# Two kinds of attention layer, interleaved: layer A's weights loaded whole, used in place, and packed into strips on the chip

## The chip, the core and the metric

The program runs on one core of one Trainium2 chip. The core has TensorE (PE, with its weight loads shown as PEld), VectorE (DVE), ScalarE (ACT), GpSimd (POOL) and SyncE (SP); each engine works through its own list of instructions in order. SP, ACT and POOL can issue transfers (DMA). The metric is the device time of one execution in microseconds (us). The time given is the median of three runs; the profile is that of one further execution, with its own time.

## The reference

The input `x` has 2048 rows of 576. Four residual layers follow each other, A, B, A, B, each on a layernorm of `x`; both A layers have the same weights, and both B layers too.

```python
# A: 32 heads of 18, each row attends to itself and 7 earlier rows, 2 apart
qkv = x @ wqkv                                   # 576 x 1728
idx = pos[:, None] - (arange(8) * 2)[None, :]    # masked where < 0
logits = einsum('bhsd,bhswd->bhsw', q, k[idx]) * 18 ** -0.5
o = einsum('bhsw,bhswd->bhsd', softmax(logits), v[idx])
out = o @ wo                                     # 576 x 576

# B: 32 heads of 128, segments of 32 rows, one after the other
mem = mem0                                       # 8 x 576
for s in range(64):
    h = concatenate([mem, xs])                   # 40 rows
    q, k, v = h @ Wq, h @ Wk, h @ Wv             # each 576 x 32 x 128
    p = softmax(mask(q @ k.T * 128 ** -0.5))     # memory sees all, rows are causal
    o = (p @ v) @ Wo                             # 32 x 128 x 576
    mem = o[:8]                                  # the next segment needs it
    outs.append(o[8:])

x = x + A(layernorm(x)); x = x + B(layernorm(x))
x = x + A(layernorm(x)); x = x + B(layernorm(x))
```

B is a recurrence: a segment's memory rows are the output of the one before.

## The kernel before

**Tiling.** The data stand transposed: features on the partitions (576 = 4 x 128 + 64, so five chunks), rows on the free axis. A works in tiles of 64 rows (`T`), B in segments of 32. Layers 1 (A) and 3 (A) and the two B layers run interleaved: step `t` of B computes segment `t` of the first B layer (lane 0) and segment `t - 5` of the second (lane 1) in the same matmuls, for 69 steps. Before a step, `trace` calls `a_tile` for the A tiles that have come due: first tile 0 alone, then tiles 1 and 2 as a pair (the "twin"), then tile 3, and from then on a tile of layer 1 with a tile of layer 3.

**Weights.** Wq, Wk and Wv of B stay in SBUF (`Wb`): 4 chunks of 128 features in a large tile each, the remaining 64 features of Wq and Wk in `wqk_r` (Wq on partitions 0 to 63, Wk on 64 to 127), those of Wv in `wv_r`. B's output weights stay in `wo`. A's weights have no tile of their own. They are used as ten strips, `[P, 5 * 256]` each: 0 to 5 are the columns of q, k and v, 6 the last 64 columns of each of the three, 7 to 9 the output projection. As long as B's output weights have not been loaded, `wo` holds the first copy of the strips ("kept", at `i * 1280`). `wload` gives a tile its strip: the first time by a gather from `A_wqkv` or `A_wo` (`L516` on SP for the four chunks, `L517` on ACT for the remainder), the second time from `wo` where it is a strip of q, k, v; later in one of two `ring` buffers, up to the third time by a gather again, which is then written to DRAM as one piece (`strips[i]`, L529), and from then on by one transfer from there (L521).

**The start.** `setup` makes the identity and the masks on POOL and the zeros on DVE. `prologue` then lists B's weight loads, all on POOL: `wqk_r` twice, the halves of Wq and Wk, those of Wv, `wv_r` twice, and `wo` in four pieces of 8 heads. The pieces of `wo` wait until what is kept there has been used. Each tile of A goes through `a_input` (load of 64 rows of x to the one buffer `x0` on SP, L660; transpose on PE, L665), `layernorm` (sums by a matmul with ones, L476; statistics on DVE; logarithm and exponential on ACT, L489 and L490), 14 blocks of projection (five matmuls each, L580), `a_attend` (products of q and k, sums over a head's 18 features by matmul, L697; softmax; spread of the weights by matmul, L722; products with v and sums), and `a_out` (L766), which adds to x, stores it, and leaves the second layernorm's result for B in `xnb`. The memory rows `mem0` are loaded to the same `x0` on SP (L448), and transposed (L452).

**A step of B.** `load_x` copies a segment to `hT`. `qk` computes q and k for the heads of a group `QG` (6, 6, 4, 6, 6, 4 heads): per head and matrix four matmuls of 128 features (L930), and one for the remaining 64. For groups in `HM` these last ones are a separate operation, in which q's and k's matmuls each use one half of the rows of the array (L949); in the other groups they are full-height matmuls (L938), in which the half that is not wanted meets zeros in `hT`. `HM` lists all six groups. `vpass` computes V (L993), `scores` the scores of 16 heads (L1034, L1038, L1044) and the softmax (`nmx`, exponential, `sum`, then a transpose to `pt`, L884), `pv` p times V (L1085), `oproj` the output (L1109), `mem_out` puts the memory rows into the next step's `hT`, and `x_out` adds to x.

**Who decides the order.** None of this is issued as it is called. `_Plan.op` records each operation with the engines that may do it, an assumed duration, a priority, what it waits for, and the buffers it takes. `_Plan.run` then plays through time with these durations, and each time an engine is free it takes the ready operation with the lowest priority number; the order so found is the order in each engine's list. On the chip an engine waits for what its next instruction needs, whatever else is ready. The priorities are numbers of `PR`; `at(t)` picks variants with `_e` or `_l` for the first 12 and last 8 steps where `PR` has them (it has none). The plan also charges 0.097 us for a change of the array's tile shape (`SWITCH`), and assumes when the weights land:

```python
return pl.op("POOL", 0.8, ..., prio, lat=max(3.0, 6.5 + mbs[0] / 0.36 - begin))
```

Of the kernel before, what the change touches and what calls it, by code (L numbers as in the profile page):

```python
# [16 lines left out]
P = 128  # L17
# [19 lines left out]
HM = ((0, 1, 2, 3, 4, 5), (0, 1, 2, 3, 4, 5))  # L37
# [11 lines left out]
class _Op:  # L49
    __slots__ = ("eng", "us", "lat", "fn", "prio", "seq", "acq", "uses", "wait", "next", "mode", "tmin", "done", "lk", "mm")  # L50


class _Plan:
# [10 lines left out]
    START = {"POOL": 8.4, "DVE": 2.5, "ACT": 2.2, "SP": 0.8}  # L64
# [190 lines left out]
class _K:  # L255
# [17 lines left out]
    def at(self, t):  # L273
        x = "_e" if t < EARLY else "_l" if t >= self.nsteps - LATE else ""
        return {k: PR.get(k + x, v) for k, v in PR.items() if k[-2:] not in ("_e", "_l")}

# [20 lines left out]
    def setup(self):  # L297
# [13 lines left out]
        self.sel(ident[:], [[-1, P]], 1, 0, ALU.is_equal, 0.0)  # L311
        self.ones = ones = cp.tile([P, P], BF16, name="ones")
# [25 lines left out]
        self.Wb = []  # L338

        qkr = cp.tile([P, NH * P], BF16, name="wqk_r")  # L340
        for nm in ("wq", "wk", "wv"):
            self.Wb.append((cp.tile([P, 4, NH * P], BF16, name=nm), cp.tile([P, (NH // 2) * P], BF16, name="wv_r") if nm == "wv" else qkr))
        self.wo = wo = cp.tile([P, NH * D + 64], BF16, name="wo")
# [52 lines left out]
        nc.vector.memset(wo[64:128, 0:9 * 1280].rearrange("p (a b) -> p a b", b=1280)[:, :, 1024:1280], 0.0)  # L396
        nc.vector.memset(wo[:, 6 * 1280:7 * 1280].rearrange("p (k n) -> p k n", n=256)[:, :, 192:256], 0.0)
        nc.vector.memset(wo[:, 9 * 1280:9 * 1280 + 640], 0.0)
# [13 lines left out]

    def prologue(self):
# [8 lines left out]
        mbs = [2.65]  # L422

        def load(out, in_, mb, begin, prio=-50.0):
            mbs[0] += mb
            return pl.op("POOL", 0.8, lambda e: nc.gpsimd.dma_start(out=out, in_=in_), prio, lat=max(3.0, 6.5 + mbs[0] / 0.36 - begin))
        src = (self.B_Wq, self.B_Wk, self.B_Wv)
        self.w_in = [[None] * 2 for _ in range(3)]
        n = 0
        for i in range(2):  # L430
            load(self.Wb[i][1][i * 64:(i + 1) * 64, :], src[i][512:576].rearrange("p h e -> p (h e)"), 0.52, 9.2 + 0.8 * n)
            n += 1
        for ws in ((0, 1), (2,)):
            for hf in range(2):
                for i in ws:
                    self.w_in[i][hf] = load(self.Wb[i][0][:, :, hf * 2048:(hf + 1) * 2048], src[i][0:512, hf * 16:(hf + 1) * 16].rearrange(
                        "(k p) h e -> p k (h e)", k=4), 2.1, 9.2 + 0.8 * n)
                    n += 1
        for hf in range(2):
            o = load(self.Wb[2][1][hf * 64:(hf + 1) * 64, :], src[2][512:576, hf * 16:(hf + 1) * 16].rearrange("p h e -> p (h e)"),  # L440
                     0.26, 9.2 + 0.8 * n)
            n += 1
        self.vr_in = o
        self.wo_in = [load(self.wo[:, n * 8 * D:(n + 1) * 8 * D].rearrange("p (h d) -> p h d", h=8),
                           self.B_Wo[n * 8:(n + 1) * 8].rearrange("h e d -> e h d"), 1.18, 36.0, -8.0) for n in range(4)]
# [49 lines left out]
    def wload(self, i, prio, dep):  # L495
# [3 lines left out]
        self.strip_n[i] = k = self.strip_n.get(i, -1) + 1  # L499
        kept = k == 0 or k == 1 and i < 7  # L500
        w = None if kept else pl.buf("ring")
        src = self.A_wqkv if i < 7 else self.A_wo
        if i < 6:
            cols = ((i // 2 * D + i % 2 * 256, 256),)
        elif i == 6:
# [19 lines left out]
        if kept:  # L525
            return view, (), self.firsts[i]
# [756 lines left out]
```

## Time and profile before

| | us |
|---|---|
| median of the runs (2100.57 to 2102.97) | 2101.82 |
| the profiled execution | 2115.16 |
| its span, first to last instruction | 2113.4 |
| PE busy in the span | 1994.7 |
| DVE busy | 1588.8 |
| ACT busy | 1094.1 |
| POOL busy | 761.8 |

Busy times are those of the profiled execution. Matmuls are pipelined, so that PE counts as busy from the first to the last of a run of them; 59,850 matmuls make its 1994.7 us. The page of the profile cuts the span in 40 equal slices and gives a digit for each, the tenths that an engine was busy. A line of the timeline has the start, the duration, the engine and source line, what is written from what, and in brackets how long the engine had been idle and what ended that. Of a transfer, the queue shows when it was issued; it lands later.

### The profile page before, as it was taken

The numbers are of one execution on the slowest core, as the hardware profiler recorded it, in microseconds if no ns is written. First come the engines' busy times: TensorE is split into PE (matmuls) and PEld (weight loads), VectorE is DVE, ScalarE is ACT, GpSimd is POOL, SyncE is SP. The second block draws the span as 40 slices with busy tenths as digits, with TensorE's granted clock in tenths as the row PEclk, the third lists the DMA queues.
The fourth block names the chain that finished last, engine by engine and source line by source line (L and its number), as shares of the span: only waits on it lengthen the run. The fifth ranks groups of instructions, "written<-read, shape, count | busy, mean of one in ns | idle before, by whom it ended". The sixth has DMA issues, their size and how long they took to land.

```text
span 2113.4 us, 130329 instructions
## 1 busy us (share of the span) xinstructions
PE 1994.7 (94%) x59850; PEld 1662.0 (79%) x59850; DVE 1588.8 (75%) x4055; ACT 1094.1 (52%) x2847; POOL 761.8 (36%) x1089
## 2 busy tenths in 40 slices
PE   0689999999999999999999999999999999999987
PEld 0567788888888888888888888887878888888776
DVE  2677778778877787778777777878777877776574
ACT  0444555555555555555555555555555555555443
POOL 2333434343343344343343433443434433322320
PEclk9889999999999999999999999999999999999998
DMA  9432222222212222222222222222222222222120
GB/s 317 140 105 58 76 78 77 72 63 70 68 55 69 78 78 76 59 76 61 56 66 78 78 77 67 68 71 59 62 70 79 77 72 62 70 68 68 58 68 10
DMA packets 92631, 161.65 MB, mean 76 GB/s; under 512 B 14632, under 2 KB 49712, under 8 KB 91952
## 3 DMA queue, kind: packets, MB, share of 16 engines
q1 hardware_dynamic: 86544, 134.14, 21.7%
q0 software_dynamic: 4576, 18.88, 2.7%
q8 instruction: 467, 7.65, 1.5%
q14 instruction: 84, 0.69, 0.1%
q10 hardware_dynamic: 960, 0.30, 0.1%
HBM read 137.32 MB, written 15.96 MB: 73 GB/s over the span
## 4 chain that ended last, share of the span: by engine, by line
PE 79%; DVE 13%; DMA 3%; issue 3%; ACT 1%; SPq 0%; DVEq 0%; POOL 0%; ACTq 0%
PE r L930 21%; PE r L1109 18%; PE r L993 17%; PE r L580 6%; DVE xn L294 4%; PE r L949 4%; PE r L1085 3%; DVE big L294 3%; PE r L766 2%; PE r L476 2%; PE r L1044 1%; DMA x<-in_B_mem_dram 1%; DVE qk L289 1%; PE r L1038 1%; PE r L697 1%
## 5 line engine op out<-in xcount | busy, mean ns | idle before, releaser
L930 PE MATMUL r<-hT,wq 128*128 128x80 bf16 (+1 forms) x8832 | 616.9, 199 | 3.4 <-issue 1.6
L930 PE MATMUL r<-hT,wk 128*128 128x80 bf16 (+1 forms) x8832 | 615.2, 199 | 0.8 <-issue 0.4
L287 ACT ACTIVATE qk<-r 128x480 bf16<-128x480 f32 (+3 forms) x610 | 267.3, 496 | 460.7 <-PE r L949 453.7
L930 PEld LDWEIGHTS <-wq 128*128 128x128 bf16 x8832 | 446.5, 100 | 28.3 <-issue 19.7
L930 PEld LDWEIGHTS <-wk 128*128 128x128 bf16 x8832 | 448.0, 100 | 1.1 <-issue 1.0
L1109 PE MATMUL r<-OT,wo 128*128 128x80 bf16 (+1 forms) x11040 | 407.8, 200 | 9.7 <-ACT OT L287 5.5
L1109 PEld LDWEIGHTS <-wo 128*128 128x128 bf16 x11040 | 394.2, 100 | 28.0 <-issue 26.0
L993 PE MATMUL r<-wv,hT 128*32 128x512 bf16 x5376 | 356.3, 383 | 3.0 <-ACT hT L287 2.3
L294 POOL TENSOR_TENSOR ex<-ex,sum 128x320 bf16<-128x320 bf16 x138 | 109.3, 792 | 593.2 <-DVE sum L874 571.6
L993 PEld LDWEIGHTS <-hT 128*32 128x32 bf16 x6720 | 164.2, 96 | 140.0 <-issue 5.2
L294 POOL TENSOR_TENSOR big<-qT,kT 128x1024 bf16<-128x1024 bf16 (+1 forms) x154 | 254.9, 1670 | 21.9 <-DVE kT L289 13.6
L294 POOL TENSOR_TENSOR big<-big 128x640 bf16<-128x640 bf16 (+1 forms) x68 | 101.6, 1494 | 358.7 <-DVE big L294 256.8
L287 ACT ACTIVATE V<-r 128x512 bf16<-128x512 f32 x275 | 164.6, 599 | 121.3 <-PE r L993 115.6
L287 ACT ACTIVATE big<-r 128x384 bf16<-128x384 f32 (+1 forms) x318 | 121.6, 437 | 136.6 <-PE r L722 135.4
L287 ACT ACTIVATE OT<-r 128x320 bf16<-128x320 f32 (+1 forms) x380 | 138.5, 422 | 88.1 <-PE r L1085 87.8
L289 DVE CAST qk<-r 128x480 bf16<-128x480 f32 (+2 forms) x218 | 122.2, 575 | 65.2 <-PE r L949 63.1
L580 PE MATMUL r<-xn,ring 128*128 128x128 bf16 (+1 forms) x2310 | 159.6, 216 | 3.2 <-issue 2.9
L863 DVE TENSOR_REDUCE nmx<-r 128x8 f32<-128x320 f32 x276 | 133.4, 483 | 32.9 <-PE r L1038 31.1
L864 DVE TENSOR_TENSOR r<-r,nmx 128x320 f32<-128x320 f32 x276 | 137.9, 500 | 9.5
L580 PEld LDWEIGHTS <-ring 128*128 128x128 bf16 x2310 | 124.7, 98 | 25.5 <-issue 15.4
L993 PE MATMUL r<-wv_r,hT 128*32 128x512 bf16 x1344 | 133.3, 380 | 0.0
L289 DVE CAST OT<-r 128x320 bf16<-128x320 f32 (+1 forms) x172 | 75.6, 461 | 71.3 <-PE r L1085 71.2
(150 smaller groups left out, 3050.3 us busy)
## 6 DMA issues: line engine op xcount, KB each, us to landing
ring<-strip SPq DMA_DIRECT2D x288, 320.0 KB, 3.2
x1T<-x SPq DMA_DIRECT2D x32, 160.0 KB, 4.3
x<-x1T SPq DMA_DIRECT2D x32, 160.0 KB, 3.0
ring<-strip SPq DMA_DIRECT2D x32, 160.0 KB, 2.3
x3T<-x SPq DMA_DIRECT2D x32, 160.0 KB, 3.3
x<-x3T SPq DMA_DIRECT2D x32, 160.0 KB, 3.9
wo<-in_B_Wo_dram POOLq DMA_DIRECT2D x4, 1152.0 KB, 8.5
wq<-in_B_Wq_dram POOLq DMA_DIRECT2D x2, 2048.0 KB, 20.7
```

Source lines behind the costliest of these rows:

```text
L287: nc.scalar.activation(out=out, in_=in_, func=ACT.Copy, scale=1.0 if scale is None else scale)
L289: (nc.vector if e == "DVE" else nc.gpsimd).tensor_copy(out=out, in_=in_)
L294: (self.nc.vector if e == "DVE" else self.nc.gpsimd).tensor_tensor(out=out, in0=in0, in1=in1, op=op)
L476: nc.tensor.matmul(psf, lhsT=(self.ones if c < 4 else self.ones_h)[:, :], rhs=xs.t[:, c].rearrange("p a t -> p (a t)"), start=(c == 0), st ...
L580: nc.tensor.matmul(ps.t[:, c * n:(c + 1) * n], lhsT=view()[:, kc, w0:w0 + P], rhs=xn.t[:, kc, 0:n], start=(kc == 0), stop=(kc == 4))
L863: nc.vector.tensor_reduce(out=m, in_=v, axis=AX.X, op=ALU.max, negate=True)
L864: nc.vector.tensor_tensor(out=v, in0=v, in1=m.unsqueeze(len(shp) - 1).to_broadcast(shp), op=ALU.add)
L930: nc.tensor.matmul(view(ps[wi])[:, hh], lhsT=self.Wb[wi][0][:, kc, h * P:(h + 1) * P], rhs=hT.t[:, kc, a:b], start=(hh == 0 and kc == 0), ...
L949: nc.tensor.matmul(view(ps[wi])[:, hh], lhsT=self.Wb[0][1][q2, h * P:(h + 1) * P], rhs=hT.t[q2, 4 + wi, a:b], start=False, stop=(hh == n - ...
L993: nc.tensor.matmul(ps.t[c * 32:(c + 1) * 32, :], lhsT=l, rhs=w, start=(kc == 0), stop=(kc == 4))
L1085: nc.tensor.matmul(ps[c].t[:, i * n + a - c0:i * n + z - c0], lhsT=V[b].t[q4, r, i, :], rhs=pt.t[q4, i, b, a:z], start=(i == 0 and b == bl ...
L1109: nc.tensor.matmul(psY.t[:, mb * W80 + c0:mb * W80 + c1], lhsT=self.wo[:, w0:w0 + P], rhs=self.OT[:, h % 16 // 4 * 8 + h // 16 * 4 + h % 4 ...
```

## The change

- `setup` makes the weight tiles before the masks, and `head` issues B's first four loads (both of `wqk_r`, the first halves of Wq and Wk) right after the identity, ahead of the masks on POOL.
- `whole` loads A's two weight matrices by four transfers on SP into `wo`, in rows of all columns, at 0 and from `WO0`. `slab` gives a tile its weights from there for the first and second use of each strip. The last 64 columns of q and k are copied side by side to `WR0` by DVE.
- `pack` copies each strip from there into a ring buffer, on POOL or DVE, and writes it to `strips[i]`. From the third use on, a strip comes from DRAM by one transfer; the gathers are gone.
- `load` lists the remaining weight loads, each in the plan only after the one eight places before has landed. The first two and the last pieces of `wo` wait for the strips packed out of them.
- `HM` has the groups 0, 1, 3 and 4, so that the groups 2 and 5 run their last 64 features at full height.
- `PR` has new numbers, and variants for tiles before the steps (`_i`), the first 5 steps (`_s`), the first 12 (`_e`) and the last 8 (`_l`). Copies of halos, some sums and products may take another engine in the first five tiles (`early`).

```diff
-HM = ((0, 1, 2, 3, 4, 5), (0, 1, 2, 3, 4, 5))
+HM = [[0, 1, 3, 4], [0, 1, 3, 4]]
...
-        x = "_e" if t < EARLY else "_l" if t >= self.nsteps - LATE else ""
-        return {k: PR.get(k + x, v) for k, v in PR.items() if k[-2:] not in ("_e", "_l")}
+        x = "_i" if t < 0 else "_s" if t < FIRST else "_e" if t < EARLY else "_l" if t >= self.nsteps - LATE else ""
+        return {k: PR.get(k + x, v) for k, v in PR.items() if k[-2:-1] != "_"}
...
         self.sel(ident[:], [[-1, P]], 1, 0, ALU.is_equal, 0.0)
...
+        self.loads = []
+        self.head()
...
+    def head(self):
+        self.mbs = 2.65
+        for i, w in ((0, self.B_Wq), (1, self.B_Wk)):
+            self.nc.gpsimd.dma_start(out=self.Wb[i][1][i * 64:(i + 1) * 64, :], in_=w[512:576].rearrange("p h e -> p (h e)"))
+            self.loads.append(0.52)
+        for i in range(2):
+            out, in_ = self.w_src(i, 0)
+            self.nc.gpsimd.dma_start(out=out, in_=in_)
+            self.loads.append(2.1)
...
+    def load(self, out, in_, mb, prio=-50.0):
+        pl, n = self.pl, len(self.loads)
+        end = self.landing(mb)
+        before = self.loads[n - 8] if n >= 8 else None
+        gate = pl.op("NONE", 0.0, None, prio, [before])
+        o = pl.op("POOL", 0.8, lambda e: self.nc.gpsimd.dma_start(out=out, in_=in_), prio, [gate], lat=3.0)
...
+        for i in range(10):
+            o = self.pack(i)
+            for n in ((0, 1) if i < 7 else (3,)):
+                pl.after(self.wo_in[n].issue, o)
...
-        kept = k == 0 or k == 1 and i < 7
...
+        kept = k < 2
+        if kept:
+            return (lambda kc, b: self.slab(i, kc, b)), (), self.firsts[2 if i == 6 else i > 6]
+        w = pl.buf("ring")
+        o = pl.op("SP", 0.5, lambda e: dma(out=w.t[:, 0:5 * n], in_=self.strips[i][:, 0:5 * n]), prio, [dep, self.strip_in[i]], acq=[w], lat=4.0)
...
-            self.first = self.firsts[i] = pl.op("SP", us, gather, -20.0 + 0.01 * i, lat=4.0)
...
+    def pack(self, i):
...
+        us = (1.15, 0.22 + 0.0004 * 5 * n) if n == 256 else (0.5, 0.3)
+        o = pl.op(("POOL", "DVE"), us, fn, PK + 0.1 * i, [self.firsts[i > 6]], acq=[w], lk=True)
+        self.strip_in[i] = pl.op("SP", 0.5, lambda e: self.nc.sync.dma_start(out=self.strips[i][:, 0:5 * n], in_=w.t[:, 0:5 * n]),
+                                 PK + 0.1 * i, [o], uses=[w], lat=5.0)
+        return o
+
+    def whole(self):
+        pl, dma = self.pl, self.nc.sync.dma_start
+        for n, (src, c0, m) in enumerate(((self.A_wqkv, 0, 3 * D), (self.A_wo, WO0, D))):
+            def main(e, src=src, c0=c0, m=m):
+                dma(out=self.wo[:, c0:c0 + 4 * m].rearrange("p (k n) -> p k n", k=4), in_=src[0:512].rearrange("(k p) n -> p k n", k=4))
+                dma(out=self.wo[0:64, c0 + 4 * m:c0 + 5 * m], in_=src[512:576])
+            self.firsts[n] = self.first = pl.op("SP", 1.3, main, -20.0 + 0.1 * n, lat=LW0 + n)
+        self.firsts[2] = pl.op("DVE", 0.4, lambda e: self.nc.vector.tensor_copy(
+            out=self.wo[:, WR0:WR0 + 5 * P].rearrange("p (k a n) -> p k a n", k=5, a=2),
+            in_=self.wo[:, 0:15 * D].rearrange("p (k a n) -> p k a n", k=5, a=3)[:, :, 0:2, 512:D]), -3.0, [self.firsts[0]])
...
-        early = jt < 2
+        early = jt < 5
...
-        if jt == 0:
-            for d in self.wo_in[:3]:
-                pl.after(d, o)
+        if self.strip_n[9] < 2:
+            pl.after(self.wo_in[3].issue, o)
...
+FIRST = 5
...
+WR0 = 24 * D
+WO0 = WR0 + 5 * P
+PK = -2.0
+LW0 = 8.5
+LB0 = 3.5
```

In the changed file the lines move: memory transpose L481, layernorm sums L505, A's projection L632, transpose of x L717, logits L749, spread L774, A's output L818, q and k L981, full-height remainders L989, half-height ones L1000, V L1044, PV L1136, output projection L1160. SP issues x (L712), the four weight transfers (L576 and L578 twice), the memory rows (L477), two strip writes (L567), and then x of tiles 1 and 2.

## The prediction, made before the changed kernel was run

> **What bounds the kernel now.** I read the page first, for where TensorE is not busy, then the busy time by window, then the timeline of the first window, then the DMA view of a stretch of it, and last the waits.
>
> ```profile
> span 2113.4 us, 130329 instructions
> ...
> PE   0689999999999999999999999999999999999987
> ...
> DMA  9432222222212222222222222222222222222120
> ```
>
> A slice is 52.8 us. PE is at 90% or more in all but three slices at the start and two at the end, and the first slice is a DMA slice. The windows give sizes (columns: window, its length, then busy us and instruction count of PE, PEld, DVE, ACT and POOL, then granted clock, DMA share, GB/s):
>
> ```profile
> 0.00:50.00 50.00, 2.34 (x30) 1.93 (x30) 11.65 (x48) 3.64 (x7) 12.69 (x31) 1.00 1.00 320
> 50.00:100.00 50.00, 29.13 (x708) 25.32 (x712) 30.05 (x92) 19.22 (x60) 13.00 (x15) 0.80 0.46 140
> 250.00:1950.00 1700.00, 1687.04 (x50051) 1409.40 (x50051) 1335.59 (x3353) 932.48 (x2391) 647.69 (x933) 1.00 0.24 69
> 1950.00:2114.00 164.00, 142.80 (x4880) 118.94 (x4864) 98.29 (x274) 67.84 (x192) 34.54 (x39) 0.95 0.17 49
> ```
>
> From 250 to 1950 us PE is idle for 13 us of 1700: that part is TensorE's own work, and a change gains there only by giving it less. What can be won is at the ends: 50 - 2.34 + 50 - 29.13 = 68.5 us idle in the first 100 us, and 21 us in the last 164. The timeline of the first 84 us says why PE starts late (start, duration, and in brackets the idle time before it and what ended it):
>
> ```profile
> 33.63 0.47 ACT L470 ACTIVATE xs<-x 128x320 bf16<-128x320 f32 x1 [21.68 <-DMA wo<-in_A_wqkv_dram]
> ...
> 47.75 1.23 PE L580 MATMUL r<-xn,wo 128*128 128x64 bf16 x20 [12.91 <-DVE xn L294]
> ...
> 52.07 0.29 PE L452 MATMUL r<-ident,x 8*128 8x8 bf16 x5 [3.10 <-DMA x<-in_B_mem_dram]
> ...
> 52.39 8.02 SPq L660 DMA_DIRECT2D x<-in_A_x_dram  x2
> ...
> 59.47 0.45 PE L665 MATMUL r<-ident,x 128*128 128x64 bf16 x5 [4.33 <-DMA x<-in_A_x_dram]
> ...
> 61.92 0.30 PE L697 MATMUL r<-big,epad 128*32 128x128 bf16 x4
> ...
> 83.55 0.29 PE L930 MATMUL r<-hT,wq 128*128 128x40 bf16 x4 [1.43 <-ACT hT L287]
> ```
>
> ACT, which issues part of A's weights, cannot go on with tile 0's layernorm[...] (21.68 us); A's first projection waits for that until 47.75, the memory rows until 52.07, tile 1's x (one x0 buffer, so only loaded after that) until 59.47; tile 0's logits at 61.92 are behind it in PE's order, and B's first matmul comes at 83.55. And why is the queue so slow? The DMA view of 20 to 46 us:
>
> ```profile
> q0 software_dynamic: 2326, 9.22, 92.3%
> q1 hardware_dynamic: 2312, 0.69, 11.4%
> ```
>
> Packets, MB, share. q0 carries B's weights from POOL, q1 what SP issues. They take turns packet for packet (2326 to 2312), at 383 GB/s together. But A's pieces here are rows of 64 or 256 columns, 128 or 512 bytes, against 4096 of B's: A gets 7% of the bytes.
>
> **The change, part by part.** The profiled execution took 2115.16 us (span 2113.4 and 1.8 around it); the median of the runs shown, 2101.82, is 13.3 less. I sum against the profile and come back to this.
>
> *(1) A's weights by four transfers, on SP alone.* SP now issues x, wqkv (512 rows of 3456 bytes), its remainder (64 rows), wo (512 of 1152), its remainder, and the memory rows. Twelve issues leave ACT, so its 21.68 us stall has no cause left. What lands when: SP's first packets flow at about 2.6 us, B's at about 3.5 (POOL now issues at 1.4 instead of 6.37, and before its first bytes came 2 us after issue). About 100 A rows go alone; the other 476 alternate with B's at 3456 + 4096 bytes a pair: 476 x 7552 / 383 GB/s = 9.4 us, and the first 128 of B's are 8192 long, 1.4 more. wqkv is in at about 15. But the memory rows are in the same queue behind wo: 576 pairs of 1152 + 4096, 7.9 us, so 23, and about 1 to land: 24. In PE's new order the memory transpose (L481) stands ahead of all of tile 0's projections (before, after the first 20), so these start at 24 too, not at 15. Then x of tile 1 is issued behind two strip writes that SP now has ahead of it (256 packets of 2560 bytes, 256 x 6656 / 383 = 4.4 us): 29, transposed, x of tile 2 at 3 us more (59.47 to 62.66 before), so logits of tile 0 at 33 against 61.92. From logits to B's first matmul I keep the 21.6 us of before (83.55 - 61.92): 55. Gain 28.5. It would be 38 if the memory rows pass wo in the queue, 20 if packets take turns less evenly.
>
> Here a rule of the Trainium skill speaks against the change. "DMA: Bandwidth & Descriptors", section "Issuing engines are not separate DMA queues", says that transfers issued from several engines run on the same DMA engines and interleave, and that starting them from several at once saves only the sequencer's time. The row above agrees on the sharing. By it, issuing B's first 5.2 MB 5 us earlier takes bandwidth from A, which now needs it first: A's 2.65 MB alone would be in at 2.6 + 2.65 / 0.383 = 9.5 us, not 23. By that rule this part loses 13 us against the best order; by the row A still lands far ahead of 47.75. I use the row.
>
> *(2) B's weights.* 16.8 MB stand ahead of the last wv_r (A's and all but B's output weights), with up to 2.3 MB of strip writes among them: 19.1 / 0.383 + 2.6 = 52 us, against B's first V pass, about 8 us after 55. Hidden, by a margin of some 10 us; without it each us late is a us of the end. POOL's two wv_r issues are now behind its first strip copy, which waits for wqkv (15): about 16.5, where they were issued at 15.4 and 18.0. B's output weights wait for the strips packed out of the same buffer and for tiles 1 and 2's projections (about 46), 4.7 MB at 383 GB/s = 12 us, so 58 for what is first needed, and o-projection came 24 us after B's first matmul (L1109 at 107.8): 79. Hidden.
>
> *(3) Strips packed on chip.* Ten copies of 128x1280, half on POOL, half on DVE, and ten writes. No row shows such a copy. DVE: between 0.36 (COPY of 32x640, L405) and 0.83 (128x1280 TENSOR_TENSOR); I take 0.7, nearer the larger size. POOL: between 0.38 (COPY 128x192) and 2.6 for the same size of TENSOR_TENSOR; 1.3. On DVE 3 come before tile 0's logits while DVE waits for x of tile 1: free. POOL's second and third wait for the ring buffer to be written (about 28 and 34), and behind them stands tile 2's xn, needed by the projection of tiles 1 and 2 at about 33 + 8.9 = 42; 34 + 1.3 + 2.4 leaves 3 us. Free, at worst 4. In exchange 30 gathers in small pieces into the ring go from SP.
>
> *(4) TensorE's work.* The orders show the same 59,850 matmuls. The groups 2 and 5 (4 heads) no longer run their remainders in half-height tiles: 1104 matmuls, at 36 ns between starts instead of a mean 17.5 (two half tiles overlap): +20.4 us. But the changes of tile shape fall from 1508 to 1339. One costs 0.1 us:
>
> ```profile
> 1970.29 0.31 PE L930 MATMUL r<-hT,wq 128*128 128x80 bf16 x4
> 1970.43 0.31 PE L930 MATMUL r<-hT,wk 128*128 128x80 bf16 x4
> 1970.67 0.53 PE L949 MATMUL r<-hT,wqk_r 64*128 64x80 bf16 x20
> ```
>
> Starts are 0.14 apart in a run of 4, 0.24 at the change. 169 x 0.1 = -16.9; up to 0.12, -20. Sum +1 (0 to +4).
>
> *(5) The new priorities* reorder all engines. Between 250 and 1950 us the waits of PE come to 9 us. In the new order the work on PE between a step's scores and its PV, the cover of the softmax, has the same median (10.9 and 7.8 us for the two halves, 10.8 and 7.9 before). The choices between engines move: by counts times the rows' means DVE gets 52 us more in all (50 evictions of 128x320 at 0.47, 26 products at 0.72, 30 sums at 0.33, less the long sums), 75% to 78% busy. Cost 0, from -6 to +25: it is a wait of 0.3 us in every step that would make 20.
>
> *(6) The stretch to 250 us* loses 31 us after 83.55 (166.5 us for 135.7 of matmul starts at full clock). The covers of the first 12 steps sum up alike in both orders; the gathers are gone. -3, from +4 to -12. *(7) The tail:* PV waits for pt (DVE L884) for 7.2 us in the last 164. The covers of the last 8 steps grow by 8 us (first half) and 12 (second) in sum: -5, from 0 to -8.
>
> Sum: -28.5 + 1 + 0 - 3 - 5 = -35.5: 2079.7 as a profiled execution. The 13.3 us between profile and median lie nowhere that I can see; taken off whole, the median is 2066. If they were lost in the transfer-bound start, the gain is smaller by a few us; I leave that to the range.
>
> **The rivals.** *A: the start is won whole.* If the memory rows do not wait behind wo, projections begin at 15 and logits at 24, some 9 us more, and with the upper ends of (6) and (7) the time is 2102 - 50 = 2052. For it: ring order is inferred, not seen. Against: in before they took from 23.6 to 52.07 behind 128-byte pieces. *B: the start stays a transfer queue.* The strip writes and x loads wait in one another's line, wqkv lands at 20 and each of the three x steps costs 2 us more: logits at 44, gain about 17 with the rest: 2085. For it: two x loads took 7 us at 52.39 under the same load. *C, slower:* DVE's 52 us fall on the softmax chain of each step, which has no free PE behind it; 52 / 69 steps = 0.75 us a step, all of it waited for: 2066 + 52 = 2118. It decides from 36 / 69 = 0.52 us a step. Against: no wait of PE on DVE of that kind between 250 and 1950, and unchanged covers. That the change does not do what it says is out: PE's order has 50 output-projection matmuls from wo where there were 25.
>
> **How the numbers follow.** My forecast 0.57 (2056 to 2078), A 0.22, B 0.14, C 0.05, and 0.02 that B and a half of C cancel the gain. Range 2044 to 2087, which takes in A and B and leaves C and a lucky steady part out. 0.2% (4 us) is about what a measurement of this kernel can tell from none: faster 0.93, same 0.02, slower 0.05.
>
> **What would show it.** Right: ACT's layernorm of tile 0 without a wait for a transfer; wqkv landing near 15 and memory rows near 24; L481 before L632 at 24; B's first matmul (L981) at 55; PE busy about 1687 in 1700 in the middle; fewer us of PV waiting for pt at the end. Wrong: projections at 15 (A), V pass or o-projection waiting for a weight (B), PV waiting for pt in the middle (C).

## The result, and the profile after

The changed kernel took 2078.04 us (median of four runs, 2076.64 to 2078.94), the kernel before on the same chip 2102.39 (now of four runs too, 2100.57 to 2106.39). The ratio is 0.9881, with a 95% interval of 0.9864 to 0.9898. The forecast was faster, 2066 us, between 2044 and 2087: the direction and the range held, the number was 12 us too low. The changed kernel's profiled execution took 2078.94 us; the sum of the prediction, against a profiled execution, was 2079.7. That agreement is partly luck, as the terms below show.

The page of the changed kernel, with the same rows as those shown of before:

```profile
span 2076.9 us, 130166 instructions
...
PE   1799999999999999999999999999999999999988
...
DMA  9532222222222122222222222222222222221220
```

The windows of the changed kernel (window, length, busy us and count of PE, PEld, DVE, ACT, POOL, granted clock, DMA share, GB/s):

```profile
0.00:50.00 50.00, 8.27 (x125) 6.93 (x126) 21.65 (x79) 8.15 (x22) 16.26 (x34) 1.00 0.97 347
50.00:100.00 50.00, 36.20 (x974) 30.14 (x974) 35.83 (x87) 20.93 (x62) 21.70 (x25) 0.87 0.59 204
...
250.00:1950.00 1700.00, 1687.94 (x50134) 1433.72 (x50130) 1357.68 (x3457) 916.55 (x2341) 606.10 (x879) 1.00 0.24 70
```

The middle is what it was (PE busy 1687.94 us of 1700, against 1687.04). The first 100 us still lose 55.5 us of PE, against 68.5. Where, the timeline of the changed kernel's start tells:

```profile
18.82 1.25 POOL L289 COPY ring<-wo 128x1280 bf16<-128x1280 bf16 x1 [6.66 <-DMA wo<-in_A_wqkv_dram]
...
20.10 9.77 SPq L567 DMA_DIRECT2D strip<-ring  x2
...
26.86 0.29 PE L481 MATMUL r<-ident,x 8*128 8x8 bf16 x5 [21.14 <-DMA x<-in_B_mem_dram]
...
27.65 0.22 DVE L511 TENSOR_SCALAR st<-r 128x64 f32<-128x64 f32 x1
...
28.31 0.47 DVE L580 COPY wo<-wo 128x640 bf16<-128x640 bf16 x1
...
28.70 0.81 DVE L289 COPY ring<-wo 128x1280 bf16<-128x1280 bf16 x1
28.98 1.26 POOL L289 COPY ring<-wo 128x1280 bf16<-128x1280 bf16 x1 [7.89 <-DMA strip<-ring]
29.43 1.21 DVE L294 TENSOR_TENSOR xn<-x,st 128x256 bf16<-128x256 f32 x2
...
29.97 8.77 SPq L712 DMA_DIRECT2D x<-in_A_x_dram  x2
...
31.09 3.36 PE L632 MATMUL r<-xn,wo 128*128 128x64 bf16 x60 [3.93 <-DVE xn L294]
...
37.80 0.45 PE L717 MATMUL r<-ident,x 128*128 128x64 bf16 x5 [3.35 <-DMA x<-in_A_x_dram]
...
44.48 0.45 PE L717 MATMUL r<-ident,x 128*128 128x64 bf16 x5 [3.78 <-DMA x<-in_A_x_dram]
...
44.85 0.72 PE L749 MATMUL r<-big,epad 128*32 128x128 bf16 x20
...
66.37 0.29 PE L981 MATMUL r<-hT,wq 128*128 128x40 bf16 x4 [2.36 <-ACT hT L287]
```

The order is the one foretold: memory rows, then A's projection, then x of tiles 1 and 2, then tile 0's logits, then B. Each station is later than foretold. A's first weights are in at 18.82 (foretold 15), when POOL's first copy of a strip stops waiting for them. Memory rows 26.86 (24): they do stand behind `wo` in SP's queue, as foretold. Projection 31.09 (24): tile 0's layernorm statistics (L511) stand on DVE behind the copies of the memory rows, and between them and `xn` stand the copies to `WR0` and to the ring, 0.47 and 0.81 us. PE is through with it before x of tile 1 comes, so it is x that holds the logits. x of tile 1 at 37.80 (29): SP's second strip write waits for a strip that DVE copies only at 28.70, so the load of x is issued at 29.97; from the issue to its transpose it takes 7.8 us, and that of tile 2 comes 6.7 later. Logits at 44.85 (33). From there to B's first matmul it is 21.5 us, as assumed (21.6).

### The profile page after: what moved, and what is told of

Read it like the earlier page. It is cut to its first block, busy times and chain, and to the rows that moved or that the text cites. A ratio compares the mean times of both kernels' runs of the same rounds, so it can differ in the third digit from the quotient of the medians.

```text
span 2076.9 us, 130166 instructions
## 1 busy us (share of the span) xinstructions
PE 1986.1 (96%) x59850; PEld 1682.9 (81%) x59850; DVE 1615.2 (78%) x4168; ACT 1080.5 (52%) x2804; POOL 714.4 (34%) x1031
## 4 chain that ended last, share of the span: by engine, by line
PE 92%; DMA 3%; DVE 2%; issue 1%; ACT 1%; SPq 0%; POOL 0%; DVEq 0%; ACTq 0%; POOLq 0%
PE r L981 30%; PE r L1044 18%; PE r L1160 18%; PE r L632 6%; PE r L1000 4%; PE r L1136 3%; PE r L818 2%; PE r L505 2%; PE r L989 2%; PE r L774 2%; PE r L1095 1%; PE r L1085 1%; DMA x<-in_B_mem_dram 1%; PE r L749 1%; PE r L1089 1%
## 5 line engine op out<-in xcount | busy, mean ns | idle before, releaser
L981 PE MATMUL r<-hT,wq 128*128 128x80 bf16 (+1 forms) x8832 | 616.0, 199 | 6.3 <-issue 3.6
L981 PE MATMUL r<-hT,wk 128*128 128x80 bf16 (+1 forms) x8832 | 615.2, 199 | 2.7 <-issue 2.7
L287 ACT ACTIVATE qk<-r 128x480 bf16<-128x480 f32 (+3 forms) x568 | 258.5, 499 | 449.4 <-PE r L1000 224.2
L981 PEld LDWEIGHTS <-wq 128*128 128x128 bf16 x8832 | 447.6, 99 | 18.6 <-issue 11.8
L981 PEld LDWEIGHTS <-wk 128*128 128x128 bf16 x8832 | 447.5, 100 | 3.0 <-issue 3.0
L1160 PEld LDWEIGHTS <-wo 128*128 128x128 bf16 x11040 | 393.9, 100 | 32.5 <-issue 27.4
L1160 PE MATMUL r<-OT,wo 128*128 128x80 bf16 (+1 forms) x11040 | 406.3, 200 | 13.4 <-ACT OT L287 6.9
L1044 PE MATMUL r<-wv,hT 128*32 128x512 bf16 x5376 | 352.9, 381 | 0.4
L1044 PEld LDWEIGHTS <-hT 128*32 128x32 bf16 x6720 | 169.5, 96 | 135.4 <-issue 0.9
L294 POOL TENSOR_TENSOR big<-big 128x1280 bf16<-128x1280 bf16 (+1 forms) x62 | 126.7, 2044 | 321.6 <-DVE big L294 163.1
L294 POOL TENSOR_TENSOR big<-qT,kT 128x1024 bf16<-128x1024 bf16 (+1 forms) x126 | 195.8, 1564 | 90.4 <-DVE oT L294 86.2
L289 DVE CAST qk<-r 128x480 bf16<-128x480 f32 (+3 forms) x260 | 138.4, 558 | 59.7 <-PE r L1000 35.9
L287 ACT ACTIVATE big<-r 128x256 bf16<-128x256 f32 (+1 forms) x257 | 98.2, 434 | 161.2 <-PE r L774 159.2
L632 PE MATMUL r<-xn,ring 128*128 128x128 bf16 (+1 forms) x2310 | 155.6, 216 | 3.9 <-issue 2.6
L632 PEld LDWEIGHTS <-ring 128*128 128x128 bf16 x2310 | 123.9, 98 | 26.2 <-issue 15.2
L1044 PE MATMUL r<-wv_r,hT 128*32 128x512 bf16 x1344 | 133.1, 379 | 0.0
L289 DVE CAST big<-r 128x256 bf16<-128x256 f32 x255 | 113.0, 485 | 19.1 <-PE r L774 17.4
```

What stands on the lines that cost most here:

```text
L287: nc.scalar.activation(out=out, in_=in_, func=ACT.Copy, scale=1.0 if scale is None else scale)
L289: (nc.vector if e == "DVE" else nc.gpsimd).tensor_copy(out=out, in_=in_)
L294: (self.nc.vector if e == "DVE" else self.nc.gpsimd).tensor_tensor(out=out, in0=in0, in1=in1, op=op)
L632: nc.tensor.matmul(ps.t[:, c * n:(c + 1) * n], lhsT=view(kc, w0), rhs=xn.t[:, kc, 0:n], start=(kc == 0), stop=(kc == 4))
L981: nc.tensor.matmul(view(ps[wi])[:, hh], lhsT=self.Wb[wi][0][:, kc, h * P:(h + 1) * P], rhs=hT.t[:, kc, a:b], start=(hh == 0 and kc == 0), ...
L1044: nc.tensor.matmul(ps.t[c * 32:(c + 1) * 32, :], lhsT=l, rhs=w, start=(kc == 0), stop=(kc == 4))
```

## The experiments

They ran in three groups (`b_again`, `a_oldnum`, `b_newnum`, `a_mem`; then `a_again`, `a_memx`, `a_lateB`, `a_HM6`; then the other four), each with the kernel before on the same chip. Its median was 2106.91, 2098.78 and 2107.76 us, and 2102.39 beside the result. So one kernel's level moves by up to 9 us from group to group: between groups ratios to before are compared, and a difference of stations is exact only within a group. "Start" in the table is A's first projection, then tile 0's logits, then B's first matmul; after it when step 6 and step 60 begin, and the end of the span, all in us of each kernel's profiled execution (the step times are those of the 1537th and 15361st matmul of q and k, of 256 in a step).

| kernel | time | ratio to before (95%) | start | step 6 | step 60 | end |
|---|---|---|---|---|---|---|
| before, first profile | 2102.39 | 1 | 47.8, 61.9, 83.5 | 258.6 | 1878.6 | 2113.4 |
| changed, first profile | 2078.04 | 0.9881 (0.9864 to 0.9898) | 31.1, 44.9, 66.4 | 231.4 | 1847.8 | 2076.9 |
| b_again | 2105.75 | 0.9993 (0.9984 to 1.0002) | 41.9, 55.5, 78.9 | 253.1 | 1870.0 | 2104.5 |
| a_oldnum | 2088.61 | 0.9908 (0.9886 to 0.9930) | 31.9, 45.7, 65.9 | 237.4 | 1853.5 | 2086.1 |
| b_newnum | 2111.92 | 1.0023 (1.0014 to 1.0032) | 37.6, 50.0, 75.3 | 264.5 | 1880.8 | 2109.6 |
| a_mem | 2073.72 | 0.9840 (0.9821 to 0.9859) | 16.7, 28.8, 54.5 | 227.3 | 1843.4 | 2070.8 |
| a_again | 2073.81 | 0.9883 (0.9868 to 0.9898) | 31.6, 45.6, 66.3 | 229.7 | 1844.9 | 2071.9 |
| a_memx | 2072.15 | 0.9872 (0.9856 to 0.9889) | 19.2, 27.5, 53.9 | 230.8 | 1845.3 | 2072.7 |
| a_lateB | 2067.37 | 0.9846 (0.9829 to 0.9862) | 15.8, 31.8, 53.2 | 220.4 | 1834.3 | 2060.6 |
| a_HM6 | 2129.71 | 1.0145 (1.0130 to 1.0160) | 31.0, 44.9, 66.3 | 236.7 | 1891.3 | 2125.2 |
| a_lateB2 | 2070.74 | 0.9826 (0.9806 to 0.9846) | 16.7, 32.2, 53.9 | 222.8 | 1838.6 | 2065.7 |
| a_late_mem | 2069.37 | 0.9820 (0.9803 to 0.9837) | 14.2, 18.2, 47.2 | 224.5 | 1840.2 | 2067.7 |
| a_memx_late | 2073.99 | 0.9841 (0.9824 to 0.9858) | 16.7, 23.3, 47.5 | 228.1 | 1844.5 | 2072.3 |
| a_oldPR | 2108.91 | 1.0012 (1.0002 to 1.0022) | 31.6, 45.2, 65.9 | 246.8 | 1872.2 | 2105.9 |

**Both kernels once more.** `b_again` is the kernel before, `a_again` the changed one, no edit.

> The kernel before, unchanged, profiled once more. If the 13 us by which its first profile (2115.16) lay above its runs are a matter of that one execution, this profile is at 2100 to 2106 and shows fewer stretches with TensorE at half clock between 130 and 215 us (three of 6.8 us in the first profile, 10 us of time). If profiling itself costs the time in the transfer-bound start, this profile is again at about 2115 and B's first matmul again at 84.

> The changed kernel once more, so that the other kernels of this group have it on the same chip, and to see how much one execution's profile of it wanders. Theory (the 13 us between the first profile of before and its median were that one execution's): median near 2078, profiled time within 5 us of the median, tile 0's projection at 31 us and B's first matmul at 66 us within 2. Rival (start-up of a profile is always dearer): profiled time 10 us or more over the median again.

The profiled execution of `b_again` took 2106.16 us, its median is 2105.75. So a profile of before is not 13 us dearer as such; that one execution was (4 of the 13 us are the levels of the two groups, and can't be placed). Its page and windows show the same middle (PE busy 1688.07 from 250 to 1950) and an earlier start:

```profile
span 2104.5 us, 130329 instructions
...
0.00:50.00 50.00, 5.41 (x85) 4.83 (x85) 14.30 (x57) 5.13 (x14) 12.65 (x31) 1.00 1.00 327
50.00:100.00 50.00, 30.09 (x722) 24.53 (x722) 30.69 (x87) 20.03 (x57) 15.87 (x18) 0.90 0.48 143
```

Of the 8.9 us between the two spans, 4.6 were lost before B's first matmul, where the transfers of A's small pieces ended 6 us later in the first (projection at 47.75 against 41.91), another 0.9 by step 6, 3.2 between steps 6 and 60, 0.3 at the end. The expectation had looked for it in stretches at half clock: the granted clock from 150 to 250 us is indeed 0.97 instead of 0.93, but only this 0.9 us shows there. The changed kernel came to its first stations within 0.7 us of the first time, and its ratio repeated; its median, 2073.81, is 4 us lower with its group.

**The loads alone, and the numbers alone.** `a_oldnum` is the changed kernel with the `PR` and `HM` of before; `b_newnum` is the kernel before with the new `PR`, the new `HM`, and the `at` that reads them.

> The changed kernel with the priorities (PR) and the head groups (HM) of before: only the start's loads, packs and slabs are new. If the gain of 24 us comes from the start, this is at 2078 to 2086, with the middle as in before. If the new numbers carry a good part (rival), it stands at 2088 to 2100. The sum on record puts 28 of 35 in the start and 7 in everything else.

> The kernel before with the priorities (PR, with their variants by stage) and the head groups (HM) of the changed kernel, and its old start. If the start carries the gain: 2096 to 2104, a little below before by the tail. If the numbers carry it (rival): 2080 to 2092. If the numbers only fit the new start: above 2105.

```diff
# a_oldnum, on the changed kernel
-HM = [[0, 1, 3, 4], [0, 1, 3, 4]]
+HM = ((0, 1, 2, 3, 4, 5), (0, 1, 2, 3, 4, 5))
-PR = dict(qk=(4.875, 5.064), ...
+PR = dict(qk=(1.315, 1.038), ...
```

The loads alone bring 0.9908, most of the gain; the numbers add some 0.0025 on top of them, 5 us (the intervals overlap in part). The time of `a_oldnum`, 2088.61, stands in the range of its rival, but that range was set at the level of the first group; the ratio is what decides. The stations place these two. Against `b_again` the loads bring 13.1 us at B's first matmul, 15.7 at step 6, 16.5 at step 60, 18.4 at the end. The numbers on top (from `a_oldnum` to the changed kernel's first profile) bring nothing at B's first matmul, 6.0 by step 6, and 9.2 at the end; the two are of different groups, so of the 9.2 only the 5 us of the ratios are safe. On the old start the same numbers lose 11.4 us by step 6 and end 0.2% slower than before: the priorities are fitted to when weights and tiles come, and are no gain by themselves. What they spare between 90 and 250 us is seen in the waits of PE in `a_oldnum` (what waited for what, us in all, times, longest); in the changed kernel the first is 0.4 us there and the last does not occur:

```profile
PE r L1136 <- DVE pt L935: 4.9, 3, 1.9
...
PE r L1089 <- DVE qk L289: 2.4, 1, 2.4
```

**Priorities and groups crossed.** `a_HM6` is the changed kernel with all six groups in half-height tiles; `a_oldPR` the changed kernel with the priorities of before and the four groups. With `a_oldnum` and `a_again` they make a square.

> The changed kernel, with all six groups of heads running their last 64 features of q and k in half-height tiles, as before. The prediction's account of TensorE (1104 full-height matmuls cost 20.4 us more, 169 fewer changes of tile shape save 17 to 20): PE's busy time from 250 to 1950 us within 4 of 1687, time within 2 us of the changed kernel. Rival 1 (a change of tile shape costs less than 0.1 us, or overlaps): 5 to 15 us faster. Rival 2 (changes cost more, or the new priorities fit the four groups only): 5 or more slower, seen as waits of PE for pt or q/k copies.

> The changed kernel with the priorities of before, but with four groups in half-height tiles (the priorities of before with all six groups and the new start gave 0.991 of before; the new ones with all six groups 1.0145). Theory 1 (the groups alone cost and bring nothing, as the prediction's account of TensorE has it; only the new priorities need the four groups): 0.989 to 0.993 of before. Theory 2 (priorities and groups fit one another both ways, since the numbers steer an order of work whose lengths the groups set): 5 to 40 us slower than that, 0.994 to 1.01, with PE waiting for copies on ACT or for pt in the middle, as with the opposite mixture.

```diff
# a_HM6
-HM = [[0, 1, 3, 4], [0, 1, 3, 4]]
+HM = [[0, 1, 2, 3, 4, 5], [0, 1, 2, 3, 4, 5]]
# a_oldPR
-PR = dict(qk=(4.875, 5.064), ...
+PR = dict(qk=(1.315, 1.038), ...
```

| ratio to before | six groups | four groups |
|---|---|---|
| priorities of before | 0.9908 | 1.0012 |
| new priorities | 1.0145 | 0.9883 |

Changing the groups alone costs 0.0262 from the changed kernel and 0.0104 from the other corner. It is not a free choice of +1 us: priorities steer an order whose lengths the groups set. Against `a_again`, `a_HM6` loses 39 of its 53 us between steps 6 and 60, mostly in TensorE's waits and not in its work. So the prediction's account of (4), by which it would have been within 2 us, does not hold for the groups alone. Its middle window and its longest waits there:

```profile
250.00:1950.00 1700.00, 1657.43 (x48940) 1386.12 (x48933) 1281.22 (x3401) 914.70 (x2322) 667.67 (x833) 0.99 0.23 68
```

```profile
PE r L1160 <- ACT OT L287: 20.9, 46, 0.6
PE r L505 <- ACT xs L499: 4.3, 5, 1.0
```

PE is idle for 43 us instead of 11 in `a_again`, half of it in 46 waits of the output projection for ACT's copies of `OT`: 0.45 us each, the small stall in each step of which the prediction had said that it would make 20 us. Up to another 8 us are the granted clock, 0.97 from 418 to 679 us, where `a_again` has 1.00 for as many matmuls (409 to 648). `a_oldPR` loses its time otherwise: PE is idle for 8.7 us only in its middle window (busy 1691.32 us), but does fewer matmuls in it (49,884; 50,189 in `a_oldnum`). Changes of tile shape in that window, counted from the trace, are 1263 in it, 1268 in `a_oldnum`, 1134 in the changed kernel. So with the old priorities the full-height remainders are paid and the shape changes do not fall; the saving that sets them off comes only with the new order. Which of the new numbers does it was not tried.

**The memory rows first.** `a_mem` loads them right after tile 0's x, into a free stretch of `wo`; the third piece of B's output weights waits for their transpose.

> The changed kernel with the memory rows loaded right after tile 0's x, ahead of A's weights in SP's queue, into a free part of wo. If the queue hands out its packets in the order of issue, the memory transpose goes from 26.9 to about 4 to 5 us, A's first projection from 31 to about 19 (when wqkv is in), and the time falls by 8 to 12 us. If something else holds the projections (x loads, weights of B), the projections come earlier and B's first matmul stays near 66; time within 3 us of the changed kernel.

```diff
+        self.pl.pool("xe", [wo[:, 16 * D + 640 * q:16 * D + 640 * (q + 1)] for q in range(1)])
-        x0, ps = pl.buf("x0"), pl.buf("r")
+        x0, ps = pl.buf("xe"), pl.buf("r")
-  ... in_=self.B_mem0[0]), -2.0, acq=[x0])
+  ... in_=self.B_mem0[0]), -29.95, acq=[x0])
+        pl.after(self.wo_in[2].issue, b)
```

A's projection starts at 16.65, held by A's weights alone; so the memory rows' place behind `wo` had cost 14 us there. B's first matmul moves by 12 us against the changed kernel's first profile, step 6 by 4 and the end by 6; these are profiles of different groups. By the ratios, 0.9840 against 0.9881 and 0.9883, the gain is some 9 us, the 8 to 12 that were expected. So a part of the 12 us is given back in the first steps, and how much, a quarter or a half, these runs don't tell.

**x of tiles 1 and 2 first, too.** `a_memx` has three such stretches, and loads x of tiles 1 and 2 into them ahead of A's weights.

> The changed kernel, with the memory rows and the rows of x of tiles 1 and 2 all loaded right after tile 0's x, ahead of A's weights, into three free stretches of the output-weight buffer (the third piece of B's output weights waits until they have been transposed). Theory (the start is a chain of small transfers, 6 to 8 us each, behind A's weights; with only the memory rows moved B's first matmul came at 54.5): projection at 17, when A's weights are in, logits of tile 0 at 25, B's first matmul at 46. Of these 20 us against the changed kernel a part is given back where step 0 now meets B's V and output weights, on their way until 52 to 58: time 2068 to 2072. Rival (step 0 is already held by B's weights when only the memory rows move): B's first matmul at 46 to 50, but V and output projection no earlier than with the memory rows alone (66 and 80), time 2073 to 2075, the same as that kernel.

```diff
-        xT, x0, ps = pl.buf("x1"), pl.buf("x0"), pl.buf("r")
+        xT, x0, ps = pl.buf("x1"), pl.buf("xe" if 0 < j < 3 else "x0"), pl.buf("r")
-                  pr(p["ai"]) if j else -30.0, [dep, self.first if j else None], acq=[x0])
+                  pr(p["ai"]) if j > 2 else -30.0 + 0.1 * j, [dep, self.first if j > 2 else None], acq=[x0])
```

The theory failed, and so did its rival, which had B's first matmul at 46 to 50. Logits come at 27.5, but B's first matmul at 53.9, half a us before that with the memory rows alone, and the end is no better: 1.7 us under the changed kernel of its group, and by the ratio not below `a_mem`. The waits of PE in the first 130 us show what takes the place of the x loads:

```profile
PE r L781 <- DVE e L294: 12.2, 2, 8.1
PE r L637 <- DMA wo<-in_A_wqkv_dram: 10.3, 2, 8.8
PE r L1167 <- DMA wo<-in_B_Wo_dram: 7.0, 1, 7.0
```

Tile 0's softmax now waits on DVE: a copy of a later strip stands ahead of it there, and waits for a ring buffer to be written. The output projection waits for B's output weights, whose third piece had to wait for the stretches.

```profile
35.18 0.82 DVE L289 COPY ring<-wo 128x1280 bf16<-128x1280 bf16 x1 [4.26 <-DMA strip<-ring]
35.92 0.28 DVE L294 TENSOR_TENSOR e<-e,sma 128x128 bf16<-128x128 bf16 x1
```

**B's first loads late.** `a_lateB` calls `head` behind the masks, `a_lateB2` is the same kernel again. This is the rule of the Trainium skill that the prediction set aside ("DMA: Bandwidth & Descriptors", section "Issuing engines are not separate DMA queues"), put to the test.

> The changed kernel, with B's first four loads issued behind the masks on POOL again, some 5 us later. Theory 1 (the rule that the prediction weighed: queues share the engines, so B's early loads take A's bandwidth): A's weights in at 10 to 12 instead of 17, memory rows transposed at 19 to 21 instead of 27, projection at 23 to 25 instead of 31, B's first matmul 5 to 8 us earlier; B's weights 5 us later are still hidden; time 3 to 6 us lower, 2072 to 2075. Theory 2 (the early loads are worth their place): start the same 5 us earlier, but B's V or output weights come 5 us later and hold step 0: V pass no earlier than 73, time 2077 to 2083.

> The changed kernel with B's first four loads behind the masks once more, so that the next two have it on the same chip: time over before's 0.983 to 0.986, as last time; projection at 16 us, logits of tile 0 at 32, B's first matmul at 53, within 2.

```diff
         self.loads = []
-        self.head()
         self.ones = ones = cp.tile([P, P], BF16, name="ones")
...
+        self.head()
         self.mem0T = mem0T = cp.tile([P, 6, NM], BF16, name="mem0T")
```

The rule was right, and the gain larger than the expectation had put it. The DMA view from 5 to 9 us of the changed kernel (packets, MB, then queue by queue packets, MB, share):

```profile
DMA packets 204, 1.00 MB, mean 249 GB/s; under 512 B 16, under 2 KB 16, under 8 KB 131
...
q0 software_dynamic: 89, 0.60, 62.6%
q1 hardware_dynamic: 115, 0.40, 40.8%
```

and the same 4 us of `a_lateB`:

```profile
DMA packets 525, 1.51 MB, mean 378 GB/s; under 512 B 31, under 2 KB 116, under 8 KB 525
...
q1 hardware_dynamic: 525, 1.51, 102.9%
```

Alone, A gets 1.51 MB in the time in which it gets 0.40 beside B's first pieces. The timeline of `a_lateB`:

```profile
12.25 0.29 PE L481 MATMUL r<-ident,x 8*128 8x8 bf16 x5 [6.52 <-DMA x<-in_B_mem_dram]
15.36 10.35 SPq L712 DMA_DIRECT2D x<-in_A_x_dram  x2
15.81 3.36 PE L632 MATMUL r<-xn,wo 128*128 128x64 bf16 x60 [3.27 <-DVE xn L294]
24.76 0.45 PE L717 MATMUL r<-ident,x 128*128 128x64 bf16 x5 [5.58 <-DMA x<-in_A_x_dram]
31.46 0.45 PE L717 MATMUL r<-ident,x 128*128 128x64 bf16 x5 [3.80 <-DMA x<-in_A_x_dram]
31.84 0.72 PE L749 MATMUL r<-big,epad 128*32 128x128 bf16 x20
```

Memory rows 12.25 instead of 27, projection 15.81 instead of 31.6, B's first matmul 53.2 instead of 66.3; B's weights, of which the first four loads are issued some 5 us later, ended one wait of PE in the first 130 us, 0.6 us for the output weights (1.6 in `a_lateB2`). Some 9 to 11 us of the 13 stay through all steps of the profiles (this execution was the fastest of its four), 6.4 us in the medians of the group (2067.37 against 2073.81), and 12 us by the ratio of `a_lateB2` (0.9826 against 0.9883). So this one-line move makes 0.9846 and 0.9826 of before; `a_mem`, with 0.9840, can't be told from it.

**Late loads together with the others.** `a_late_mem` is `a_mem` with the call moved, `a_memx_late` is `a_memx` with it moved.

> B's first four loads behind the masks, and the memory rows loaded right after tile 0's x (the two single edits gave 6 us and about 8 us). Theory (what is left in front is still the chain of small loads): the memory rows are in at 4, tile 0's projection starts when A's weights are in, 11 to 13; x of tile 1 now stands directly behind A's weights in the queue and is in before 15, x of tile 2 at 22 to 24, logits of tile 0 at 22 to 25, B's first matmul at 44 to 47; half of these 7 us stays, 3 to 5 us off the kernel with late loads. Rival (step 0 is now held by B's weights, which arrive no earlier): B's first matmul at 44 to 47, but its V pass or output projection waits for a weight, and the time is the same within 2 us or higher.

> B's first four loads behind the masks, and the memory rows and x of tiles 1 and 2 ahead of A's weights. Theory: projection at 12 to 14, logits at 18 to 20, B's first matmul at 40 to 44, but the output projection of step 0 waits for B's output weights (7 us with the early loads): time within 3 us of the kernel with late loads. Rival (with A's weights in earlier, the packs and so the output weights move up too): no wait for them, 5 to 8 us faster than the kernel with late loads.

Projections at 14.2 and 16.7, logits at 18.2 and 23.3, B's first matmul at 47.2 and 47.5, 6 to 7 us before the late loads alone; and at the end nothing of it can be measured (0.9820 and 0.9841, against 0.9826). The waits of PE in the first 130 us name the new bound in `a_late_mem`:

```profile
PE r L1047 <- DMA wv_r<-in_B_Wv_dram: 4.3, 1, 4.3
```

and `a_memx_late` waits 4.9 us there and 6.7 for the output weights. So what holds step 0 now is the stream of weights itself, the 16.8 MB that end with V's, as the rival in the expectation of `a_late_mem` had it: an earlier start of A runs into it. The rest of the 6 us goes in the V pass behind that wait. First `a_late_mem`, then `a_lateB`; the windows are those in which PE runs the pass:

```profile
62.30 0.54 PE L1047 MATMUL r<-wv_r,hT 128*32 128x512 bf16 x4 [4.29 <-DMA wv_r<-in_B_Wv_dram]
63.61 1.90 PE L1047 MATMUL r<-wv,hT 128*32 128x512 bf16 x16 [0.77 <-ACT V L287]
62.00:70.00 8.00, 6.93 (x86) 2.57 (x88) 1.54 (x5) 2.59 (x6) 0.67 (x2) 0.57 1.02 395
```

```profile
66.06 1.03 PE L1044 MATMUL r<-wv,hT 128*32 128x512 bf16 x16
64.00:72.00 8.00, 7.88 (x168) 3.55 (x160) 5.37 (x11) 3.90 (x8) 3.67 (x6) 0.90 0.69 261
```

At a granted clock of 0.57 instead of 0.90 it does half the matmuls in 8 us, and the pass is over at 72.5 and 72.3: nothing is left of the start that was 6 us earlier.

## Why the prediction was right or wrong

**The 13.3 us.** This step decided the number. The prediction summed -35.5 us against the first profile, reached 2079.7, and then took off the whole 13.3 us by which that profile lay above the median, since they "lie nowhere that I can see". `b_again` shows where 8.9 of them lay: 4.6 in the transfer-bound start, the very part that the change replaces, 0.9 from there to step 6, and 3.2 in the steps behind. A loss in a part that is removed must not be subtracted again: the 28.5 of (1), read from the first profile's 83.55, holds the 4.6 already. Against `b_again` the terms come to -27.6, 8 less than foretold, and more than half of these 8 us are this double count; the others are terms mis-sized. The medians differ by 24.4; the last 3 us are the level of the group in which `b_again` ran. The prediction named the possibility of a double count and left it to the range.

**The terms**, foretold, against the first profile of before, and against `b_again`, which ran at its median:

| term | foretold | against the first profile | against b_again |
|---|---|---|---|
| (1) start, to B's first matmul | -28.5 | -17.2 | -12.6 |
| (6) from there to step 6, about 250 us | -3 | -10.0 | -9.1 |
| (4) and (5) steps 6 to 60 | +1 | -3.7 | -0.5 |
| (7) from step 60 on | -5 | -5.6 | -5.4 |
| sum | -35.5 | -36.5 | -27.6 |

That the sum of the first profile comes to within 1 us is luck: (1) is 11 us too large, (6) is 7 too small, and 3.2 us of the middle are that one execution's.

(1) had the right mechanism and was mis-sized by 11.3 us, on the way to the memory rows and from there to the logits. The memory rows came 2.9 us later, of which a part is the rate of 249 GB/s beside B's first pieces instead of 383. From them to tile 1's x it took 10.9 us instead of 5: SP's second strip write, which stands ahead of the load, waits for a copy on DVE that stands behind those of the memory rows, and the load itself takes 7.8. Tile 2's x took 6.7 instead of 3, and the rest of the way to B 1 us less than foretold. These 3 us were read at 59.47 to 62.66 of before, when the other queue was running dry; the same load took 6.6 in `b_again` (53.02 to 59.66). "These start at 24 too", of the projections, left out the same order of DVE and was wrong by 7 us, but PE waited for x after them, so this is no part of the 11.3.

Rival B had named the x loads, from the two at 52.39, and its "logits at 44" came true (44.85). Its total does not follow from it: logits at 44 make the start 18 us shorter, with the rest of the sum 25, which is 2077 and not 2085. Nor does rival A's: the start, 9 us more, and the upper ends of (6) and (7) make 56.5, which is 2045 and not 2052.

(6) was under-sized, inside its range of +4 to -12. From B's first matmul to step 6 `a_oldnum` takes 171.5 us, the changed kernel 165.0 and 163.4, `a_HM6` 170.4 and `a_oldPR` 180.9: so some 6 us of it are the new priorities together with the four groups, and neither alone. The prediction had costed them at nothing under (5).

(7) was right in size, and its waits went the way foretold, in the changed kernel's last 127 us:

```profile
PE r L1136 <- DVE pt L935: 4.6, 5, 1.2
```

against 7.2 before, in the last 164. `b_newnum` has the short tail on the old start (228.8 us from step 60 on, `b_again` 234.5), and `a_oldnum` not (232.6): it comes from the new numbers. (4) is right for the pair of changes (PE's middle 1687.94 against 1687.04, and 1339 changes of tile shape in all, as foretold), but for neither alone. Rival C did not happen: DVE grew by 26 us in all, half of the 52 foretold, and PE's waits for it in the middle come to 0.5 us.

(2) was wrong in one piece. V's weights were in time, and three pieces of B's output weights too, but the last one, tied to the second use of A's output strips, was issued at 90.11, behind a softmax product on POOL:

```profile
90.11 0.93 POOL L441 DMA_DIRECT2D wo<-in_B_Wo_dram  x1
...
99.04 0.22 PE L1160 MATMUL r<-OT,wo 128*128 128x48 bf16 x1 [3.35 <-DMA wo<-in_B_Wo_dram]
```

3.3 us of PE. (3) had the sizes: 0.81 on DVE (0.7 foretold) and 1.26 on POOL (1.3). "Free" was wrong: x of tile 1 is queued behind the write that waits for DVE's copy, two copies of 1.3 us stand ahead of `xn`, and POOL's copy slows `xn` itself (last section).

**The rule against the row.** The prediction read correctly that by the rule the early loads cost A 13 us, and said that A would still land "far ahead of 47.75". That compares with the old kernel and not with what the new one needs next: measured, the early loads cost 15.2 us at the memory rows (27.43 in `a_again`, 12.25 in `a_lateB`) and 6 to 12 us at the end.

## What to carry to other kernels

A start made of small loads behind big ones is a chain of queue places: put what is needed first, first in its queue, and hold back other engines' big loads until it is through; a load that shares the DMA engines is not free because another engine issues it. Then look for what will bind next: with both moves the start came 6 us earlier, and the wait for V's weights and a lower granted clock behind it took it back. Before taking the difference between a profile and the median off a sum, take a second profile: if the excess lies in the part that the change removes, it must not be counted twice. Priorities fitted to a planned order belong to that order, so an edit that changes a length in a planned order is measured with both.

## What the runs showed of the hardware

Rows of 8192 bytes, which B's first loads write to 64 partitions, were slow. In `a_lateB` from 12 to 15 us nothing else moves, and they make 221 GB/s with all 16 DMA engines busy:

```profile
DMA packets 97, 0.66 MB, mean 221 GB/s; under 512 B 16, under 2 KB 16, under 8 KB 16
q0 software_dynamic: 97, 0.66, 101.2%
```

A's rows of 3456 bytes alone made 378 in the view of 5 to 9 us. Beside B's first rows they were slowed as well: 0.40 MB in 40.8% of 4 us is 245 GB/s. The prediction had costed these 128 rows at the rate of all others. Whether it is the size of a row or the 64 partitions was not tried.

Products on DVE were slower while POOL copied a strip. The first two of tile 0's `xn` took 1.21 us together in the changed kernel, with POOL's copy from 28.98 to 30.24 beside them, and 0.54 in `a_lateB`, where POOL's copy was over (12.10 to 13.37). Tile 1's took 1.60 at 46.49, with POOL's next copy from 46.74 to 48.01:

```profile
14.82 0.54 DVE L294 TENSOR_TENSOR xn<-x,st 128x256 bf16<-128x256 f32 x2
```

The granted clock differs between executions of one program. The window from 50 to 100 us of `a_again` has 0.77, where the changed kernel's first profile has 0.87; PE is busy 1.2 us longer there, for nearly the same number of matmuls:

```profile
50.00:100.00 50.00, 37.38 (x971) 29.93 (x971) 35.88 (x89) 21.16 (x62) 21.95 (x25) 0.77 0.59 205
```

In this window the changed kernel and its variants have 0.74 to 0.88. In the V pass of `a_late_mem` a part of what an earlier start wins is given back to the clock, as shown above; how much it is in the other versions stays open.
